# DMA transposes of one head at a time with two buffers each way, the last pair turned on TensorE, and new numbers in the scheduler

## The chip, the cores and the metric

One core of a Trainium2 chip runs the whole program. The metric is device time in microseconds (us), the median of three runs. A profile of one more execution shows what each engine did: PE (TensorE matmuls), PEld (its weight loads), DVE (VectorE), ACT (ScalarE), POOL (GpSimd) and SP, the engine that issues every DMA here.

## The reference

Attention with a compressive memory, over 4 batches, 8 heads, 576 positions and 64 elements a head, and then one gated feed-forward layer over the 2304 rows that come out:

```python
scores = scale * np.matmul(q, k.transpose(0, 1, 3, 2))
scores = np.where(causal, -1000000000.0, scores)
a = np.exp(scores - scores.max(-1, keepdims=True))
local = np.matmul(a / (a.sum(-1, keepdims=True) + 1e-09), v)
mem_out = einsum(phi(q), M_prev) / (einsum(phi(q), z_prev) + 1e-06)
x = g * mem_out + (1 - g) * local          # g is a gate per head
...
gate = 1.0 / (1.0 + np.exp(-(x @ w_gate)))   # 512 by 1536
val = x @ w_val                              # 512 by 1536
out = gate * val @ w_out                     # 1536 by 512
```

## The kernel before, in words

**Groups and pairs.** The 2304 rows are worked on in six groups of 384. Groups 1 to 4 are the first 384 positions of a batch; groups 0 and 5 ("tails") are the last 192 positions of two batches each. A group has four pairs of heads, so there are 24 pairs, numbered 0 to 23; a pair has three items of 128 query rows.

**Attention of a pair.** `scores` multiplies queries and keys on PE into a PSUM bank, reduces them on DVE into `a` (with the running extreme in `st`), and takes the exponential on ACT. `turn` brings `a` of an item into `at`, with keys on the partitions: for pairs below `XBAR` (8) by PE transposes (`transpose`) and ACT copies; from pair 8 on through `crossed`. That one splits the 32-bit numbers into two planes of 16 bits on DVE (into `pl`), has SP issue a DMA transpose (`tl<-pl`), and puts the planes together on DVE (`at<-tl`). `values` multiplies `at` with the values (tiles `vt` and `vr`) on PE, `scaled` divides, the memory term is added (`xs`), and `across` transposes `xs` on PE into `xh` and `xl`, high and low parts of the expert's input. An item has one block of 128 keys, two or three in groups 1 to 4; in group 5 it has four, four and five (the fifth half filled).

**Expert.** `moe(g)` runs over 12 slices of 128 hidden columns. A slice takes 24 matmuls with 384 columns (`wg` and `sv` with `xh` and `xl`) and nine with 512 columns (`sv` with `gh` and `gl`). The weights are converted once, in group 0, from 64-bit numbers that are loaded into `wr`, written to a scratch tensor and loaded again as `sv` in each later group. Attention of group g + 1 is laid beside `moe(g)`; the first slice of a group puts the blocks of x that come last (those of the fourth pair) at its end. Group 0's attention has almost no expert work beside it, and the last group's expert work has no attention beside it.

**Order.** All instructions go through `Program.add`, with an engine, a cost in us, what is read and written, and `kb` for transfers. `Program.issue` plays the program through by these costs: on each engine it takes the ready instruction with the lowest place in the program, less a `LEAD` by part and engine. What comes out is the order on each engine, and each engine runs it in that order and waits where its data is not there. So a cost that is changed moves instructions on all engines. SP too issues in that order; a transfer that waits for its source holds up those behind it.

**Buffers of the turn.** `pl` and `tl` are rings (`Ring`) of one buffer each, 2048 numbers of 16 bits wide. They lie in `wr0` and `wr1`, which nobody needs any more when the weights are converted.

Of the kernel before, what the change touches and what calls it, by code (L numbers as in the profile page):

```python
# [29 lines left out]

LEAD = {("attention", "pe"): 150, ("weights", "sp"): 200}

# [9 lines left out]
class Program:  # L42
# [7 lines left out]
    def __init__(self):  # L50
        self.ops = []
        self.writer = {}
        self.readers = {}
        self.touched = {}
        self.before = {}
        self.part = ""
        self.turn = None

    def renew(self, key):

        last = self.touched.get(key)
# [87 lines left out]
def tile_attention_memory_moe(  # L149
# [26 lines left out]
    class Ring:  # L176
# [10 lines left out]
        def take(self):  # L187
            i = self.at % self.n
            self.at += 1
            tag, lies = self.tags.get(i, (f"{self.name}{i}", None))  # L190
            k = pg.renew(lies or (self.name, i))
            if i not in self.tiles:
                self.tiles[i] = sb.tile(self.shape, self.dtype, name=f"{self.name}{i}", tag=tag)
                if self.init:
                    self.init(self.tiles[i], k)
            return self.tiles[i], k
# [11 lines left out]
    def pe(cost, emit, r, w):  # L208
        pg.add("pe", cost, emit, r, w)
# [5 lines left out]
    def product(out, lhsT, rhs, n, r, w, start, stop):  # L215
        pe(0.06 if n <= 100 else 4 * n / 2385.0,
           lambda: nc.tensor.matmul(out=out, lhsT=lhsT, rhs=rhs, start=start, stop=stop), r, w)  # L217
# [73 lines left out]
    def pad(t, k):  # L291
# [14 lines left out]
    vt_r = Ring("vt", [128, 5, 2, VC], F32, 2)  # L306
    kp_r = Ring("kp", [128, 2 * GT], F32, 4)
    kq_r = Ring("kq", [128, 2 * GT], F32R, 5,
                {0: ("wr2", ("wr", 2)), **{i + 1: (f"wt{i}", ("wt", i)) for i in range(4)}})
    ql_r = Ring("ql", [128, GT], F32R, 2, init=half)  # L310
    a_r = Ring("a", [128, 640], F32, 5, init=pad)
    st_r = Ring("st", [128, 2], F32, 6)
    at_r = Ring("at", [128, 1280], F32, 4)
    pl_r = Ring("pl", [128, 4 * DM], U16, 1, {0: ("wr0", ("wr", 0))})
    tl_r = Ring("tl", [128, 4 * DM], U16, 1, {0: ("wr1", ("wr", 1))})
    xs_r = Ring("xs", [128, 3, 2, D], F32, 2)
# [138 lines left out]
    def scores(n, c):  # L455
# [8 lines left out]
        def part(i, k0, k1):  # L464
# [32 lines left out]
        for (aj, ak), (sj, sk) in zip(a, st):  # L497
            act(W, lambda aj=aj, sj=sj: nc.scalar.activation(  # L498
                out=aj[:, :W], in_=aj[:, :W], func=AF.Exp, scale=-1.0, bias=sj[:, len(ns) - 1:len(ns)],
            ), [ak, sk], [ak])  # L500
        u.a[c] = a

    def crossed(a, nb, at, k):


        W = 128 * nb
        keys = []
        for js in [(0, 1)] if nb < 5 else [(0,), (1,)]:
            m = len(js)
            pl, pk = pl_r.take()  # L510
            tl, lk = tl_r.take()
            pks = [pk + (j,) for j in js]
            for x, j in enumerate(js):
                t, ak = a[j]
                src = t[:, :W].bitcast(U16).rearrange("p (w two) -> p two w", two=2)
                dst = pl[:, 2 * W * x:2 * W * (x + 1)].rearrange("p (two w) -> p two w", two=2)
                dve(2 * W, lambda src=src, dst=dst: nc.vector.tensor_copy(out=dst, in_=src),  # L517
                    [ak] + [ak[:2] + (ak[2], "pad")] * (nb == 5), [pks[x]], fast=True)
            src, dst = pl[:, :2 * W * m], tl[:, :2 * W * m].rearrange("p (x q) -> p x q", q=128)
            pg.add("sp", 0.5, lambda src=src, dst=dst: nc.sync.dma_start_transpose(out=dst, in_=src),  # L520
                   pks, [lk], 1.05 * W * m)
            src = tl[:, :2 * W * m].rearrange("p (m two w) -> p m two w", m=m, two=2)
            dst = at[:, W * js[0]:W * js[0] + W * m].bitcast(U16).rearrange("p (m w two) -> p m two w", m=m, two=2)
            if m == 1:
                src, dst = src[:, 0], dst[:, 0]
            key = k + (js[0],)
            dve(2 * W * m, lambda src=src, dst=dst: nc.vector.tensor_copy(out=dst, in_=src), [lk], [key], fast=True)  # L527
            keys.append(key)
        return keys

    def turn(n, c):
# [60 lines left out]

    def attn():
        load_pair(0)
        gates()
        load_values(0)
# [252 lines left out]
```

## Time and profile before

| | before |
|---|---|
| median of three runs | 682.6 us (682.58 to 683.85) |
| profiled execution, its own time | 682.01 us |
| span of its instructions | 680.2 us |
| PE busy | 644.5 us (95%) |
| PEld busy | 561.6 us (83%) |
| DVE busy | 428.9 us (63%) |
| ACT busy | 297.9 us (44%) |
| POOL busy | 12.1 us (2%) |
| mean granted TensorE clock | 0.982 |

The span goes from the first instruction to the last; the execution's own time is 1.8 us longer. A busy share is a mean over all stages. Matmuls overlap in the records, so that a busy PE says only that it was not waiting. In tables by stretch each engine has its busy us and, in brackets, its number of instructions, in the order PE, PEld, DVE, ACT, POOL; behind them stand the granted TensorE clock (1.00 is 2.4 GHz, 0.50 is 1.2 GHz), the mean busy share of the 16 DMA engines, and GB/s. In a timeline "xN" is a run of N like instructions, and square brackets give the idle time of the engine before it and what ended it.

### The profile page before, as it was taken

The numbers are of one execution on the slowest core, as the hardware profiler recorded it, in microseconds if no ns is written. First come the engines' busy times: TensorE is split into PE (matmuls) and PEld (weight loads), VectorE is DVE, ScalarE is ACT, GpSimd is POOL, SyncE is SP. The second block draws the span as 40 slices with busy tenths as digits, with TensorE's granted clock in tenths as the row PEclk, the third lists the DMA queues.
The fourth block names the chain that finished last, engine by engine and source line by source line (L and its number), as shares of the span: only waits on it lengthen the run. The fifth ranks groups of instructions, "written<-read, shape, count | busy, mean of one in ns | idle before, by whom it ended". The sixth has DMA issues, their size and how long they took to land.

```text
span 680.2 us, 12091 instructions
## 1 busy us (share of the span) xinstructions
PE 644.5 (95%) x4744; PEld 561.6 (83%) x4744; DVE 428.9 (63%) x1110; ACT 297.9 (44%) x580; POOL 12.1 (2%) x52
## 2 busy tenths in 40 slices
PE   4999999999999999999999999999999999289997
PEld 2556688888799999999998998988998987279996
DVE  6787879889837755666676476578467675321112
ACT  5777657648625433543344344336234333011111
POOL 2000000000000000000000000000000000000000
PEclk9999999999999999999999999999999999579999
DMA  8777748877797657786776988677976769304542
GB/s 292 257 245 239 223 137 282 269 261 247 207 254 206 191 167 236 228 188 198 202 194 178 265 214 198 175 209 242 240 192 187 192 184 266 70 10 177 186 147 85
DMA packets 97097, 138.44 MB, mean 204 GB/s; under 512 B 72720, under 2 KB 74768, under 8 KB 87824
## 3 DMA queue, kind: packets, MB, share of 16 engines
q1 hardware_dynamic: 97040, 137.67, 68.3%
q8 instruction: 37, 0.61, 0.4%
q14 instruction: 20, 0.16, 0.1%
HBM read 104.09 MB, written 17.30 MB: 178 GB/s over the span
## 4 chain that ended last, share of the span: by engine, by line
PE 90%; DVE 4%; DMA 3%; ACT 1%; issue 1%
PE bank L213 71%; PE bank L217 10%; PE bank L477 5%; PE bank L220 3%; DMA tl<-pl 2%; DVE a L489 1%; DVE pl L517 1%; DMA wr<-in_w_dram 1%; ACT a L498 1%; DVE at L527 1%; DMA kp<-in_qk_dram 0%; DVE kq L236 0%; DVE xs L236 0%; ACT xh L226 0%; DVE gl L236 0%
## 5 line engine op out<-in xcount | busy, mean ns | idle before, releaser
L213 PE MATMUL bank<-xh,wg 128*128 128x384 f32 x576 | 166.0, 344 | 0.6 <-ACT xh L226 0.6
L213 PE MATMUL bank<-xh,sv 128*128 128x384 f32 x576 | 163.2, 340 | 0.0
L213 PE MATMUL bank<-sv,gh 128*128 128x512 f32 x432 | 139.7, 399 | 0.0
L725 DVE SCALAR_TENSOR_TENSOR th<-th,bank 128x384 f32<-128x384 f32 x72 | 39.8, 552 | 124.1 <-PE bank L213 117.6
L213 PEld LDWEIGHTS bank<-xh,wg 128*128 128x128 f32 x576 | 106.3, 190 | 5.8 <-issue 1.7
L213 PEld LDWEIGHTS bank<-xh,sv 128*128 128x128 f32 x576 | 105.6, 188 | 2.2 <-issue 1.6
L498 ACT ACTIVATE a<-a,st 128x512 f32<-128x512 f32 (+4 forms) x144 | 81.9, 583 | 39.2 <-DVE st L489 38.5
L213 PE MATMUL bank<-xl,wg 128*128 128x384 f32 x288 | 98.6, 342 | 0.0
L213 PE MATMUL bank<-xl,sv 128*128 128x384 f32 x288 | 98.4, 342 | 0.0
L213 PEld LDWEIGHTS bank<-sv,gh 128*128 128x128 f32 x432 | 79.0, 188 | 13.8 <-issue 1.8
L723 ACT ACTIVATE th<-bank 128x384 f32<-128x384 f32 x72 | 35.3, 490 | 125.4 <-PE bank L213 125.4
L213 PE MATMUL bank<-sv,gl 128*128 128x512 f32 x216 | 86.0, 398 | 0.0
L226 ACT CAST gh<-th 128x384 fp32r<-128x384 f32 x72 | 36.8, 512 | 105.4 <-DVE th L725 105.3
L489 DVE CUSTOM_DVE_ANT_0 a<-bank,mask 128x128 f32<-128x128 f32 (+4 forms) x144 | 68.5, 486 | 14.4 <-PE bank L213 5.9
L226 ACT CAST kq<-kp 64x768 fp32r<-64x768 f32 (+1 forms) x76 | 48.0, 638 | 27.3 <-PE bank L213 25.9
L527 DVE COPY at<-tl 128x512 uint16<-128x512 uint16 (+4 forms) x52 | 45.1, 867 | 21.8 <-DMA tl<-pl 21.5
L213 PEld LDWEIGHTS bank<-xl,wg 128*128 128x128 f32 x288 | 54.7, 190 | 3.4 <-issue 0.5
L213 PEld LDWEIGHTS bank<-xl,sv 128*128 128x128 f32 x288 | 54.3, 188 | 1.2 <-issue 0.7
L236 DVE TENSOR_TENSOR gl<-th,gh 128x384 fp32r<-128x384 f32 x72 | 40.0, 556 | 22.0 <-ACT gh L226 21.4
L477 PE MATMUL bank<-kp 64*128 64x512 f32 (+5 forms) x156 | 44.1, 491 | 8.8 <-DMA kp<-in_qk_dram 8.8
L213 PEld LDWEIGHTS bank<-sv,gl 128*128 128x128 f32 x216 | 40.6, 188 | 8.4 <-issue 0.2
L517 DVE COPY pl<-a 128x256 uint16<-128x256 uint16 (+4 forms) x96 | 44.2, 495 | 0.1
(65 smaller groups left out, 716.6 us busy)
## 6 DMA issues: line engine op xcount, KB each, us to landing
sv<-w SPq DMA_DIRECT2D x60, 1024.0 KB, 5.1
wr<-in_w_dram SPq DMA_DIRECT2D x36, 512.0 KB, 4.8
kp<-in_qk_dram SPq DMA_DIRECT2D x32, 384.0 KB, 5.0
w<-sv SPq DMA_DIRECT2D x12, 1024.0 KB, 5.8
out_dram<-ob SPq DMA_DIRECT2D x14, 256.0 KB, 5.5
vt<-in_vp_dram SPq DMA_DIRECT2D x8, 330.0 KB, 4.8
vr<-in_vp_dram SPq DMA_DIRECT2D x8, 330.0 KB, 4.1
vt<-in_vp_dram SPq DMA_DIRECT2D x8, 198.0 KB, 2.9
```

The costliest lines, as they stand in the source:

```text
L213: lambda: nc.tensor.matmul(out=out, lhsT=lhsT, rhs=rhs, start=start, stop=stop), r, w)
L217: lambda: nc.tensor.matmul(out=out, lhsT=lhsT, rhs=rhs, start=start, stop=stop), r, w)
L220: pe(0.110, lambda: nc.tensor.transpose(out=out, in_=in_, identity=identity), r, w)
L226: act(n, lambda: nc.scalar.copy(out=out, in_=in_), r, w)
L236: dve(n, lambda: nc.vector.tensor_tensor(out=out, in0=in0, in1=in1, op=op), r, w)
L477: pe(2 * m / 2385.0, lambda kp=kp, j=j, r=r, q=q, m0=m0, m1=m1: nc.tensor.matmul(out=sp[j][0][m0:m1, :m], lhsT=kp[r, u.qa + q:u.qa + q + m ...
L489: dve(m + 60, lambda aj=aj, sj=sj, pj=pj: nc.vector.tensor_tensor_reduce(out=aj[:, k0:k1], in0=pj[:, :m], in1=mk, scale=-0.125, scalar=3.0 ...
L498: act(W, lambda aj=aj, sj=sj: nc.scalar.activation(out=aj[:, :W], in_=aj[:, :W], func=AF.Exp, scale=-1.0, bias=sj[:, len(ns) - 1:len(ns)], ...
L517: dve(2 * W, lambda src=src, dst=dst: nc.vector.tensor_copy(out=dst, in_=src), [ak] + [ak[:2] + (ak[2], "pad")] * (nb == 5), [pks[x]], fas ...
L527: dve(2 * W * m, lambda src=src, dst=dst: nc.vector.tensor_copy(out=dst, in_=src), [lk], [key], fast=True)
L723: act(GT, lambda: nc.scalar.activation(out=th, in_=pg_[:, :GT], func=AF.Tanh, scale=0.5), [pg_k], [th_k])
L725: dve(GT, lambda: nc.vector.scalar_tensor_tensor(out=th, in0=th, scalar=1.0, in1=pv[:, :GT], op0=ALU.add, op1=ALU.mult,), [th_k, pv_k], [t ...
```

## The change

- `crossed` turns one head at a time: two DMA transposes for an item where there was one (or, for an item of five blocks, two of five blocks), each with its own copy out. `pl` and `tl` become rings of two buffers of half the width; both halves of `pl` lie in `wr0` and both of `tl` in `wr1`.
- The fifth block of a tail's item goes through PE transposes and an ACT copy (key `"end"`).
- The last pair (23) is turned on PE, as pairs 0 to 7 are.
- The loads of pair 0's keys and queries (`kp`) get a lead of 1000 on SP, and stand ahead of the first weights.
- Costs in the scheduler: a narrow product 0.068 for 0.06, score matmuls of the first nine pairs up by 0.07 or 0.21 each, exponentials by 0.1 (120 columns), the issue of a DMA transpose 1.3 for 0.5, and its transfer 1.5 KB a column of a head for 1.05.
- The rings' keys are tracked so that a buffer laid into another's place has its own name; nothing is computed in another way.

```diff
-LEAD = {("attention", "pe"): 150, ("weights", "sp"): 200}
+LEAD = {("attention", "pe"): 150, ("weights", "sp"): 200, ("first", "sp"): 1000}
...
-        pe(0.06 if n <= 100 else 4 * n / 2385.0,
+        pe(0.068 if n <= 100 else 4 * n / 2385.0,
...
-    pl_r = Ring("pl", [128, 4 * DM], U16, 1, {0: ("wr0", ("wr", 0))})
-    tl_r = Ring("tl", [128, 4 * DM], U16, 1, {0: ("wr1", ("wr", 1))})
+    pl_r = Ring("pl", [128, 2 * DM], U16, 2, {i: (plain, "wr", 0) for i in range(2)})
+    tl_r = Ring("tl", [128, 2 * DM], U16, 2, {i: (turned, "wr", 1) for i in range(2)})
...
-                        pe(2 * m / 2385.0, lambda kp=kp, j=j, r=r, q=q, m0=m0, m1=m1: nc.tensor.matmul(
+                        pe(2 * m / 2385.0 + (0.07 if pair else 0.21), lambda kp=kp, j=j, r=r, q=q, m0=m0, m1=m1: nc.tensor.matmul(
...
-            act(W, lambda aj=aj, sj=sj: nc.scalar.activation(
+            act(W + 120, lambda aj=aj, sj=sj: nc.scalar.activation(
...
-        W = 128 * nb
+        n = min(nb, 4)
+        W = 128 * n
         keys = []
-        for js in [(0, 1)] if nb < 5 else [(0,), (1,)]:
-            m = len(js)
+        for j, (t, ak) in enumerate(a):
             pl, pk = pl_r.take()
             tl, lk = tl_r.take()
...
-            pg.add("sp", 0.5, lambda src=src, dst=dst: nc.sync.dma_start_transpose(out=dst, in_=src),
-                   pks, [lk], 1.05 * W * m)
...
+            pg.add("sp", 1.3, lambda pl=pl, tl=tl: nc.sync.dma_start_transpose(
+                out=tl.rearrange("p (x q) -> p x q", q=128), in_=pl), [pk], [lk], 1.5 * W)
...
+        if nb > n:
+            tp, tk = bank("att")
+            for j, (t, ak) in enumerate(a):
+                transpose(tp[:, j * 128:j * 128 + 128], t[:, W:W + 128], idn,
+                          [ak, "idn", ak[:2] + (ak[2], "pad")], [tk])
+            key = k + ("end",)
+            copy(at.rearrange("p (j x) -> p j x", j=2)[:, :, W:W + 128],
+                 tp[:, :256].rearrange("p (j x) -> p j x", j=2), 256, [tk], [key])
             keys.append(key)
...
-        if n >= XBAR:
+        if XBAR <= n < NP - 1:
...
+        pg.part = "first"
         load_pair(0)
+        pg.part = "attention"
```

**Where instructions stand.** The first transfers on SP, before (`wr` are weights, `kp` keys and queries, `bt` the gate's numbers):

```order
L244 DMA wr_129<-in_w_dram 128x1024
L244 DMA wr_131<-in_w_dram 128x1024
L244 DMA wr_133<-in_w_dram 128x1024
L244 DMA kp_101<-in_qk_dram 128x768
L244 DMA kp_102<-in_qk_dram 128x768
L244 DMA bt<-in_beta_dram 128x8
```

and of the change (its line 256 is line 244 of before):

```order
L256 DMA kp_101<-in_qk_dram 128x768
L256 DMA kp_102<-in_qk_dram 128x768
L256 DMA wr_129<-in_w_dram 128x1024
L256 DMA wr_131<-in_w_dram 128x1024
L256 DMA wr_133<-in_w_dram 128x1024
L256 DMA bt<-in_beta_dram 128x8
```

The two loads of pair 0 went ahead of three weight loads; from `bt` on the first 19 transfers stand as before.

On PE, where the last pair's attention ends, before (`kq` and `ql` are its last scores; `vr` with `at` its values; bank_66 and bank_67 with `xh_154` the first slice of the last group):

```order
L213 MATMUL bank_66<-xh_154,wg_89 128x384
L213 MATMUL bank_67<-xh_154,sv_128 128x384
L213 MATMUL bank_67<-xl_155,sv_128 128x384
L213 MATMUL bank_67<-xh_154,sv_128 128x384
L213 MATMUL bank_68<-kq_164 128x256
L213 MATMUL bank_68<-kq_164,ql_161 128x256
L213 MATMUL bank_68<-kq_162 64x256
L213 MATMUL bank_68<-kq_162,ql_161 64x256
L217 MATMUL bank_69<-vr_110,at_127 64x66 x16
L217 MATMUL bank_69<-vr_111,at_137 64x66 x16
```

and of the change (lines 225, 229 and 232 are 213, 217 and 220 of before; `a` is what is transposed; `xh_140` belongs to the group before the last):

```order
L225 MATMUL bank_67<-xl_141,sv_150 128x384
L232 MATMUL bank_68<-idn,a_118 128x128
L232 MATMUL bank_68<-idn,a_119 128x128 x3
L225 MATMUL bank_67<-xh_140,sv_150 128x384 x2
L225 MATMUL bank_67<-xl_141,sv_150 128x384
L225 MATMUL bank_67<-xh_140,sv_150 128x384
L225 MATMUL bank_63<-sv_145,gh_148 128x512 x2
L229 MATMUL bank_70<-vr_110,at_127 64x66 x16
L229 MATMUL bank_70<-vr_111,at_137 64x66 x16
```

The last pair's values stood behind everything else that PE could do, with only the rest of the last group after them; now they stand inside the last two slices of the group before, and the 26 new transposes of that pair lie in runs of one to four between its matmuls. A little further on, with the pair's `xs`:

```order
L225 MATMUL bank_65<-sv_145,gl_149 128x512
L225 MATMUL bank_63<-sv_150,gh_152 128x512 x2
L225 MATMUL bank_63<-sv_150,gl_153 128x512
L232 MATMUL bank_68<-idn,xs_143 128x128 x3
L225 MATMUL bank_64<-sv_150,gh_152 128x512 x2
L225 MATMUL bank_64<-sv_150,gl_153 128x512
L225 MATMUL bank_65<-sv_150,gh_152 128x512 x2
L225 MATMUL bank_65<-sv_150,gl_153 128x512
L225 MATMUL bank_66<-xh_154,wg_89 128x384
```

Ten matmuls with 512 columns now stand between the last value product and the transposes of `xs`, and six of them and 18 of the next group's first slice behind those, ahead of the first that needs them.

In groups 1 to 4 SP had one transpose for an item, as here:

```order
L520 DMA_TRANSPOSE tl_159<-pl_158 128x12x128
L244 DMA sv_128<-w_80 128x2048
L520 DMA_TRANSPOSE tl_159<-pl_158 128x4x128
L244 DMA vt_103<-in_vp_dram 128x396
L244 DMA sv_145<-w_81 128x2048
```

and has two of the change, between the same loads:

```order
L530 DMA_TRANSPOSE tl_wr_159<-pl_wr_158 128x6x128 x2
L256 DMA out_dram<-ob_156 64x512 x2
L256 DMA sv_128<-w_80 128x2048
L530 DMA_TRANSPOSE tl_wr_159<-pl_wr_158 128x2x128 x2
L256 DMA vt_103<-in_vp_dram 128x396
```

There are 52 DMA transposes before, and 90 of the change; PE has 32 transposes more.

## Rows read from the trace of the kernel before

**Rows 1.** stretches of the whole program: us, then busy us (instructions) by engine
```profile
8.26:85.00 76.74, 71.56 (x753) 44.70 (x753) 63.24 (x194) 55.88 (x112) 1.67 (x12) 1.00 0.74 248
85.00:570.97 485.97, 485.67 (x3479) 437.14 (x3477) 334.89 (x857) 221.52 (x432) 6.01 (x20) 1.00 0.74 213
...
577.00:600.30 23.30, 6.82 (x109) 5.75 (x108) 9.03 (x16) 1.60 (x3) 0.00 (x0) 0.59 0.30 59
600.30:605.30 5.00, 5.00 (x15) 4.57 (x16) 1.65 (x3) 1.01 (x2) 0.00 (x0) 0.50 0.00 0
605.30:675.30 70.00, 69.91 (x365) 64.83 (x363) 12.98 (x24) 11.88 (x25) 0.00 (x0) 1.00 0.38 136
```

**Rows 2.** what PE's matmuls waited for: us in total, times, longest us
```profile
PE bank L477 <- DMA kp<-in_qk_dram: 8.8, 2, 8.3
PE bank L217 <- issue: 7.5, 2, 5.7
PE bank L217 <- DVE at L527: 6.5, 2, 3.6
```

**Rows 3.** timeline before the last group: start us, us, engine, line, instruction
```profile
579.97 12.68 SPq L520 DMA_TRANSPOSE tl<-pl  x3
584.27 1.31 DVE L527 COPY at<-tl 128x2048 uint16<-128x2048 uint16 x1 [4.33 <-DMA tl<-pl]
...
595.59 1.37 PE L217 MATMUL bank<-vr,at 128*64 128x66 f32 x20 [3.61 <-DVE at L527]
...
598.83 0.90 PE L220 MATMUL bank<-idn,xs 128*128 128x128 f32 x3 [1.88 <-DVE xs L236]
...
600.30 0.69 PE L213 MATMUL bank<-xh,wg 128*128 128x384 f32 x1 [0.57 <-ACT xh L226]
```

**Rows 4.** stretch 570.97 to 605.30, only the matmuls of L213
```profile
570.97:605.30 34.33, 10.24 (x43) 8.85 (x44) 0.65 0.41 92
```

**Rows 5.** chain that ended last, two pieces: start us, us, what
```profile
16.60 1.05 PE bank L477 x2
...
533.43 3.18 PE bank L217 x104
```

**Rows 6.** timeline of PE in the middle and before the hole
```profile
345.09 0.49 PE L220 MATMUL bank<-idn,xs 128*128 128x128 f32 x3
345.33 0.48 PE L213 MATMUL bank<-sv,gh 128*128 128x512 f32 x1
...
571.25 0.34 PE L213 MATMUL bank<-xh,wg 128*128 128x384 f32 x1
571.42 0.34 PE L213 MATMUL bank<-xh,sv 128*128 128x384 f32 x1
```

**Rows 7.** timeline of the first 24 us
```profile
0.74 1.34 SPq L244 DMA_DIRECT2D wr<-in_w_dram  x3
...
4.74 0.66 ACT L639 ACTIVATE wt<-wr 128x512 f32<-128x512 f32 x1 [2.72 <-DMA wr<-in_w_dram]
...
7.31 3.69 SPq L244 DMA_DIRECT2D mb<-in_mz_dram  x4
...
8.26 3.52 PE L477 MATMUL bank<-kp 64*128 64x512 f32 x8 [8.26 <-DMA kp<-in_qk_dram]
...
16.10 0.39 PE L217 MATMUL bank<-mb,ph 128*128 128x130 f32 x2
```

**Rows 8.** loads of tile mb in the first 20 us
```profile
DMA to landing us min/median/max: 5.3/6.5/7.5
```

**Rows 9.** tile tl: durations ns min/median/max, and from issue to landing
```profile
L520 SPq DMA_TRANSPOSE tl<-pl x52: 1190/1366/7332, 175.2 to 591.3; - x52
L527 DVE COPY at<-tl x52: 455/890/1367, 185.3 to 594.7; 128x512 uint16<-128x512 uint16 x12, 128x1024 uint16<-128x1024 uint16 x12, 128x1536 uint16<-128x1536 uint16 x12, 128x2048 uint16<-128x2048 uint16 x8
...
DMA to landing us min/median/max: 2.4/4.9/9.4
```

**Rows 10.** tile at, copies from PSUM: ns min/median/max
```profile
L226 ACT COPY at<-bank x44: 353/577/599, 13.9 to 166.5; 128x512 f32<-128x512 f32 x32, 128x256 f32<-128x256 f32 x12
```

More of the change, by code (lines that the diff above doesn't have):

```diff
@@ L55, in __init__ @@
         self.before = {}
+        self.closed = set()
         self.part = ""
@@ L59, in renew @@
     def renew(self, key):
+        assert key not in self.closed, f"{key} has a new tenant"
         last = self.touched.get(key)
@@ L189, in take @@
             self.at += 1
-            tag, lies = self.tags.get(i, (f"{self.name}{i}", None))
-            k = pg.renew(lies or (self.name, i))
+            k = pg.renew((self.name, i))
             if i not in self.tiles:
-                self.tiles[i] = sb.tile(self.shape, self.dtype, name=f"{self.name}{i}", tag=tag)
+                home = self.tags.get(i)
+                if home:
+                    hosts, ring, at = home
+                    if hosts[at] is None:
+                        hosts[at] = sb.tile([128, hosts["wide"]], self.dtype, name=f"{self.name}_{ring}{at}", tag=f"{ring}{at}")
+                    place = sum(1 for j in self.tiles if self.tags.get(j) == home) * self.shape[1]
+                    self.tiles[i] = hosts[at][:, place:place + self.shape[1]]
+                    pg.before[(self.name, i)] = set(pg.touched[(ring, at)][1]) | pg.before[(self.name, i)]
+                    pg.closed.add((ring, at))
+                else:
+                    self.tiles[i] = sb.tile(self.shape, self.dtype, name=f"{self.name}{i}", tag=f"{self.name}{i}")
                 if self.init:
@@ L307, in tile_attention_memory_moe @@
     kp_r = Ring("kp", [128, 2 * GT], F32, 4)
+    in_wr, in_wt = {"wide": 2 * GT, 2: None}, {"wide": 2 * GT, **dict.fromkeys(range(4))}
+    plain, turned = {"wide": 4 * DM, 0: None}, {"wide": 4 * DM, 1: None}
     kq_r = Ring("kq", [128, 2 * GT], F32R, 5,
-                {0: ("wr2", ("wr", 2)), **{i + 1: (f"wt{i}", ("wt", i)) for i in range(4)}})
+                {0: (in_wr, "wr", 2), **{i + 1: (in_wt, "wt", i) for i in range(4)}})
     ql_r = Ring("ql", [128, GT], F32R, 2, init=half)
@@ L503, in crossed @@
     def crossed(a, nb, at, k):
-        W = 128 * nb
+        n = min(nb, 4)
+        W = 128 * n
         keys = []
-        for js in [(0, 1)] if nb < 5 else [(0,), (1,)]:
-            m = len(js)
+        for j, (t, ak) in enumerate(a):
             pl, pk = pl_r.take()
             tl, lk = tl_r.take()
[L512 to L519, printed above, removed]
-            pg.add("sp", 0.5, lambda src=src, dst=dst: nc.sync.dma_start_transpose(out=dst, in_=src),
-                   pks, [lk], 1.05 * W * m)
[L522 to L527, printed above, removed]
@@ new lines, in crossed @@
+            pl, tl = pl[:, :2 * W], tl[:, :2 * W]
+            src = t[:, :W].bitcast(U16).rearrange("p (w two) -> p two w", two=2)
+            dve(2 * W, lambda src=src, pl=pl: nc.vector.tensor_copy(
+                out=pl.rearrange("p (two w) -> p two w", two=2), in_=src), [ak], [pk], fast=True)
+            pg.add("sp", 1.3, lambda pl=pl, tl=tl: nc.sync.dma_start_transpose(
+                out=tl.rearrange("p (x q) -> p x q", q=128), in_=pl), [pk], [lk], 1.5 * W)
+            dst = at[:, 128 * nb * j:128 * nb * j + W].bitcast(U16).rearrange("p (w two) -> p two w", two=2)
@@ new lines, in crossed @@
+            key = k + (j,)
+            dve(2 * W, lambda tl=tl, dst=dst: nc.vector.tensor_copy(
+                out=dst, in_=tl.rearrange("p (two w) -> p two w", two=2)), [lk], [key], fast=True)
+            keys.append(key)
+        if nb > n:
[6 more added lines that the diff above has]
+                 tp[:, :256].rearrange("p (j x) -> p j x", j=2), 256, [tk], [key])
```

## The prediction

> **What bounds the kernel now.** I read the table by stretches first. From 85.00 to 570.97 PE is busy 485.67 of 485.97 us at a clock of 1.00 [rows 1]: there PE is the bound, the other engines have slack (DVE 334.89 of 485.97), and an edit is worth what it adds to or takes from PE. Two places are different. Before 8.26 PE does nothing, and from there to 85.00 it is idle 5.2 us (76.74 less 71.56) [rows 1]; the waits of PE's matmuls say that the 8.26 is a wait for the first keys [rows 2]. And from 577.00 to 605.30 the rest is lost: 6.82 busy us in 23.30 at a mean clock of 0.59, and then 5.00 us at 0.50 [rows 1]. The timeline of that hole shows who holds PE: three DMA transposes of the last pair one after another, each followed by a copy of DVE that waited for it, then value products that waited for the copy, the pair's `xs`, and at 600.30 the first expert matmul that needs it [rows 3]. Nothing else was left for PE: the group before had run out, and so had those 18 matmuls of the next first slice that don't need the fourth pair. From 605.30 on PE runs 365 matmuls in 70.00 us without a gap [rows 1], and stores end the program; neither is touched.
>
> **How large the hole is.** From 570.97, where the values of pair 22 end, to 605.30 pass 34.33 us. The useful work in it at full clock: 43 matmuls of L213 [rows 4], at the 0.17 us from one start to the next that full-clock neighbours show (571.25, 571.42) [rows 6], 7.3; 104 value products in 3.2, as for an earlier pair [rows 5]; six transposes, at three in 0.24 (345.09 to 345.33) [rows 6], 0.5. Together 11.0, so 23.3 us are lost. Of these 2.4 are the clock alone: 15 matmuls in 5.00 us [rows 1] would take 2.6.
>
> **The last pair on PE** takes that hole away, if PE has other work while the pair's chain runs. In the new order the pair's values stand inside the last two slices of the group before; ten matmuls with 512 columns cover the way from its values to its `xs` (at some 0.23 each, by 0.17 for 384 columns, 2.3 us; in the hole that way took from 596.96, where the products ended, to 598.83 [rows 3], 1.9), and six more and the 18 of the next slice cover the rest. I take back all 23.3, and leave 1.0 for waits in that stretch: none at the least, and at most those of the second rival below. PE never falls idle for long, so I expect the clock to stay at 1.00.
>
> **Added work on PE.** 26 transposes for the last pair and six for the fifth blocks of pairs 20 to 22. In the steady stretch one costs 0.08 us [rows 6]; some stand alone or in twos, so I take 0.09, and 2.9 in all. Bounds: 2.6 at 0.08, and 9.6 if each took the 0.30 of the three at half clock (0.90) [rows 3], to which I give little, since these run at full clock. The Trainium skill, "TensorE: Matmul & The Clock Gate", Part 4: PE-mode transpose, gives about 275 ns for one of 128 by 128 inside a kernel, and would make this term 8.8 and the time 667; the spacing of 0.08 here decides against it, so it has no chance of its own below. The ten copies to `at` that go with them take ACT 0.58 each [rows 10], 5.8 us of an engine that is busy 221.52 of 485.97 [rows 1]; only the last one stands on a path, and its cover is the six expert matmuls ahead of the values.
>
> **Halves instead of whole items** for pairs 8 to 22. SP issues 90 transposes for 52; at 1.37 us each [rows 9] the 38 more cost SP 52 us, spread over the 416 from the first to the last [rows 9]. Behind a transpose that waits for DVE stand weight loads, and PE waits for these; the cover is that `sv` has three buffers. DVE makes 38 copies more out of `tl`, each at half the width; even at the shortest now, 0.46, [rows 9] that is 17 us less the wider ones that go, inside 151 us of slack. From issue to landing a transpose takes 2.4 to 9.4 us, 4.9 in the median, over sizes of one to four [rows 9], so a half is hardly quicker than the whole, but with two buffers the second is on its way 1.4 us behind the first. I take nothing for all this; it gains nothing because PE doesn't wait there, and what it can cost is the first rival. The Trainium skill speaks against cutting transfers, in "DMA: Bandwidth & Descriptors", by its two cost components: about 2.0 us fixed, and then bytes over 436 GB/s. The shortest landing here, 2.4, agrees with it; 38 more would be 76 us of waiting if they stood one behind another on the path, and 661 would become 737.
>
> **First keys first.** The first weights landed at 4.74, when ACT took them up, 4.0 us after SP's first issue; the keys behind three weight loads let PE start at 8.26 [rows 7]. In their place the keys land by about 4.4 (they are smaller), so PE starts 3.9 earlier at the most. But bytes ahead of the later loads are the same, and the memory term that follows needs `mb`, issued in four parts from 7.31 on, in 3.69 us [rows 7], and landing 5.3 to 7.5 later [rows 8], the last near 15.5; PE used it at 16.10 [rows 7]. There PE meets the data again. By then the change has put two more score matmuls, 1.05 us [rows 5], ahead of it, and the remaining wait is 0.6 to 1.0 shorter: I take 2.0. The ends are 0 and 3.9. On DVE and ACT the first conversions move back by some 2 us behind the first scores; these weights are wanted only when group 0's expert work starts.
>
> **Other costs** move instructions on every engine. Where PE is full that can't help; up to 85.00 there are 5.2 idle us to win, or as many to lose if a wait moves. I take 0, with 2 either way.
>
> **The sum** against the profiled execution: 682.0 − 23.3 + 1.0 + 2.9 − 2.0 = 660.6. That execution is 0.6 below the median of the runs, so 661.2, and I say **661**.
>
> **Rivals.** *The halves come late* (the other side). If the second half waits for the first to land, an item's turn is longer by up to 4.9 − 1.4 = 3.5 us [rows 9], and the third item of each of 15 pairs (8 to 22) is the one that its values wait for. For: landing does not shrink with size, and the order leaves the values little beyond the time that the scheduler assumes. Against: the halves have a buffer each, and PE hardly waits now from 85.00 to 570.97 (0.3 us) [rows 1] with landings as uneven as 2.4 to 9.4. All of it would be 15 × 3.5 = 52 us: 713, slower. It decides from 1.4 us a pair on, where 15 × 1.4 eats the 21.4 won. In a mild form, the three tail pairs alone waiting 2 to 3 us, it gives 668.
>
> *The last pair's chain is not covered.* If the group before is through earlier than the order assumes, PE still waits for the pair: for the way from values to the first expert matmul, 596.96 to 600.30 [rows 3], 3.3; a copy of 0.6 [rows 10]; and reduction and exponential ahead of it, which I estimate at as much again as the way behind. That is 7 us where I left 1: 667. For it: all of it is one serial chain. Against: 10, 6 and 18 matmuls stand in its gaps.
>
> *The change does not empty the hole*, because pairs 20 to 22, still turned by DMA, end as late as they did: then only the last pair's own three waits go (7.5 and 6.5 us of idle time [rows 2]) less the transposes: about 670.
>
> *The first keys give nothing*: 663; *or all*: 659.
>
> **How the numbers follow.** The forecast with either end of the first keys 0.70; the uncovered chain 0.12; late halves, mild, 0.07; a hole that stays in part 0.05; late halves in all pairs 0.04; no change within 0.2% (1.4 us, about what runs of this kernel tell from nothing) 0.02. From the terms the forecast's own range is 656 (all of the keys, nothing left to wait, 2 won early) to 665; up to 669 it takes in the uncovered chain and the mild late halves, and that leaves out about 1 in 10. Faster 0.94, same 0.02, slower 0.04.
>
> **What the profile after would show.** Hole: no stretch of clock 0.50 behind 85 us, and no idle time of PE above 1 us between the pair's last scores and the last group's first slice; value products of the last pair waiting for ACT's copy, if for anything. Keys: PE's first matmul near 4.4, its first with `mb` near 15, and the first expert matmul about 2 us earlier. Transposes: 0.08 to 0.11 apart. Halves: PE's idle time in the middle still under 1 us, with landings near 4 and SP waiting less for `tl<-pl`. The prediction is wrong if PE waits for copies out of `tl` at the values of pairs 8 to 22, or if weight loads land late behind waiting transposes.

## The result and the profile after

The changed kernel takes **659.37 us** (median of 4 runs, 657.28 to 662.13), the kernel before 682.59 in the runs beside it. The ratio is 0.966, 95% interval [0.962, 0.970]: faster by 3.4%. The profiled execution took 662.13 us, the slowest of the four; its span is 660.3. The forecast was 661, in a range of 656 to 669.

The page of after, engine totals and then busy tenths and granted clock in 40 slices of the span:

```profile
PE 639.6 (97%) x4776; PEld 561.7 (85%) x4776; DVE 423.2 (64%) x1142; ACT 303.9 (46%) x590; POOL 9.1 (1%) x52
...
PE   5998999999999999999999999999999999999996
...
PEclk9899989999999999999999999999999999999999
```

Each digit is a slice of 16.5 us. There is no hole in the tail any more; the clock is below 9 tenths only in the second and the sixth slice. The windows of after, cut at its own events (us, PE busy, instructions, granted clock, DMA share, GB/s), answer to [rows 1]:

```profile
0.00:8.26 8.26, 4.37 (x11) 1.00 0.74 253
8.26:12.24 3.98, 3.51 (x27) 1.00 0.90 334
12.24:15.95 3.71, 0.00 (x1) 0.93 1.08 259
15.95:20.00 4.05, 4.05 (x12) 0.50 0.95 325
20.00:85.00 65.00, 59.11 (x699) 0.97 0.74 242
85.00:565.27 480.27, 478.65 (x3469) 1.00 0.75 211
565.27:579.41 14.14, 14.14 (x173) 1.00 0.18 64
579.41:600.30 20.89, 20.78 (x113) 1.00 0.61 213
600.30:654.95 54.65, 54.65 (x286) 1.00 0.39 139
```

Two things stand here. From 565.27 on, where 22 of the last pair's 26 transposes begin (four ran at 547.94), PE is never idle for more than 0.11 us in a row of the table, at full clock; before, 23.30 us held 6.82 busy ones at 0.59. And the start has a new gap: 3.71 us without work, and behind it 4.05 us at 0.50. The 1.00 in the first row is no reading: the trace of after has no entry of the clock before 8.60 us, and where there is none the table prints 1.00. What PE's matmuls waited for in the whole program (us in total, times, longest; the first three) answers to [rows 2]:

```profile
PE bank L491 <- DMA kp<-in_qk_dram: 7.6, 2, 3.8
PE bank L491 <- DVE xs L248: 1.7, 2, 0.9
PE bank L225 <- ACT xh L238: 1.4, 1, 1.4
```

The waits of value products for copies out of the transposed tile (6.5 and 7.5 before) are gone. The wait for first keys is now two, 3.8 at the start of the program and 3.7 for the second pair's keys. PE's timeline in the tail (start, us, instruction) answers to [rows 3]; L225, L229 and L232 are L213, L217 and L220 of before:

```profile
568.26 0.60 PE L232 MATMUL bank<-idn,a 128*128 128x128 f32 x4
568.62 0.42 PE L225 MATMUL bank<-xh,sv 128*128 128x384 f32 x1
568.88 0.60 PE L232 MATMUL bank<-idn,a 128*128 128x128 f32 x4
...
569.49 0.34 PE L225 MATMUL bank<-xl,sv 128*128 128x384 f32 x1
569.67 0.34 PE L225 MATMUL bank<-xh,sv 128*128 128x384 f32 x1
...
571.55 0.62 PE L225 MATMUL bank<-sv,gh 128*128 128x512 f32 x2
572.10 3.25 PE L229 MATMUL bank<-vr,at 128*64 128x66 f32 x104
...
577.68 0.49 PE L232 MATMUL bank<-idn,xs 128*128 128x128 f32 x3
...
579.41 0.33 PE L225 MATMUL bank<-xh,wg 128*128 128x384 f32 x1
```

The reader sees the pair's chain laid into expert matmuls: transposes in fours, the 104 value products at 572.10, `xs` at 577.68, and the last group from 579.41. No row has a wait in brackets. `xs` stands 21.15 us earlier than the 598.83 of [rows 3]. Four transposes take 0.36 (568.26 to 568.62), and the matmul behind them 0.26 to the next start (568.62 to 568.88) where one between matmuls takes 0.18 (569.49 to 569.67): 0.44 for a run of four, 0.11 each.

The turned tile of after (durations ns min/median/max, first and last start; from issue to landing) answers to [rows 9]:

```profile
L530 SPq DMA_TRANSPOSE tl_wr<-pl_wr x90: 1167/1220/3065, 169.4 to 549.0; - x90
...
DMA to landing us min/median/max: 2.3/4.8/8.5
```

In the median a half lands no sooner than a whole did (4.9), with two buffers and so at times two transposes under way. The first 20 us, SP's issues and then PE, answer to [rows 7, 8]:

```profile
0.73 0.88 SPq L256 DMA_DIRECT2D kp<-in_qk_dram  x2
1.65 1.38 SPq L256 DMA_DIRECT2D wr<-in_w_dram  x3
...
4.89 1.38 SPq L256 DMA_DIRECT2D kp<-in_qk_dram  x2
7.88 4.85 SPq L256 DMA_DIRECT2D mb<-in_mz_dram  x4
```

```profile
3.85 3.78 PE L491 MATMUL bank<-kp 64*128 64x512 f32 x8 [3.85 <-DMA kp<-in_qk_dram]
...
15.95 2.08 PE L491 MATMUL bank<-kp 64*128 64x512 f32 x4 [3.71 <-DMA kp<-in_qk_dram]
17.96 0.80 PE L229 MATMUL bank<-mb,ph 128*128 128x130 f32 x2
```

PE begins 4.4 us earlier than before and then stands still for the second pair's keys; `mb` is used at 17.96, not at 16.10. The first eight scores take 3.78, near the pace of the four behind the gap, which take 2.08 at 0.50.

### The profile page after: what moved, and what is told of

It reads as the page before. It is cut to its first block, busy times and chain, and to the rows that moved or that the text cites. A ratio compares the mean times of both kernels' runs of the same rounds, so it can differ in the third digit from the quotient of the medians.

```text
span 660.3 us, 12262 instructions
## 1 busy us (share of the span) xinstructions
PE 639.6 (97%) x4776; PEld 561.7 (85%) x4776; DVE 423.2 (64%) x1142; ACT 303.9 (46%) x590; POOL 9.1 (1%) x52
## 4 chain that ended last, share of the span: by engine, by line
PE 86%; DMA 6%; DVE 4%; ACT 2%; issue 1%; SPq 1%; ACTq 0%; DVEq 0%
PE bank L225 72%; PE bank L229 8%; PE bank L491 3%; DMA kp<-in_qk_dram 3%; PE bank L232 3%; DMA wr<-in_w_dram 2%; DMA tl_wr<-pl_wr 2%; DVE a L503 1%; SPq L256 1%; DVE wt L662 0%; ACT a L512 0%; DVE wt L665 0%; DVE ql L248 0%; DVE kq_wt L248 0%; DVE xl L248 0%
## 5 line engine op out<-in xcount | busy, mean ns | idle before, releaser
L225 PE MATMUL bank<-xh,wg 128*128 128x384 f32 x576 | 165.4, 342 | 1.9 <-ACT xh L238 1.4
L225 PE MATMUL bank<-xh,sv 128*128 128x384 f32 x576 | 164.2, 341 | 0.2 <-DVE th L744 0.2
L225 PE MATMUL bank<-sv,gh 128*128 128x512 f32 x432 | 142.9, 400 | 0.0
L225 PEld LDWEIGHTS bank<-xh,wg 128*128 128x128 f32 x576 | 105.3, 188 | 8.7 <-issue 2.1
L225 PEld LDWEIGHTS bank<-xh,sv 128*128 128x128 f32 x576 | 104.9, 188 | 2.3 <-issue 1.1
L225 PE MATMUL bank<-xl,sv 128*128 128x384 f32 x288 | 98.2, 341 | 0.0
L225 PE MATMUL bank<-xl,wg 128*128 128x384 f32 x288 | 97.6, 339 | 0.2 <-DVE xl L248 0.2
L225 PEld LDWEIGHTS bank<-sv,gh 128*128 128x128 f32 x432 | 78.9, 188 | 12.1 <-issue 0.8
L225 PE MATMUL bank<-sv,gl 128*128 128x512 f32 x216 | 86.0, 398 | 0.0
L225 PEld LDWEIGHTS bank<-xl,wg 128*128 128x128 f32 x288 | 54.3, 189 | 3.4 <-issue 0.5
L534 DVE COPY at<-tl_wr 128x256 uint16<-128x256 uint16 (+3 forms) x90 | 46.5, 519 | 14.0 <-DMA tl_wr<-pl_wr 13.6
L225 PEld LDWEIGHTS bank<-xl,sv 128*128 128x128 f32 x288 | 54.1, 188 | 1.2 <-issue 0.7
L238 ACT CAST kq_wt<-kp 64x768 fp32r<-64x768 f32 (+2 forms) x60 | 38.1, 637 | 24.7 <-PE bank L225 22.8
L225 PEld LDWEIGHTS bank<-sv,gl 128*128 128x128 f32 x216 | 40.6, 188 | 8.5 <-issue 0.7
L491 PE MATMUL bank<-kp 64*128 64x512 f32 (+5 forms) x156 | 38.1, 511 | 9.8 <-DMA kp<-in_qk_dram 7.6
L528 DVE COPY pl_wr<-a 128x256 uint16<-128x256 uint16 (+3 forms) x90 | 41.8, 469 | 0.1
```

The costliest lines, as they stand in the source:

```text
L238: act(n, lambda: nc.scalar.copy(out=out, in_=in_), r, w)
L491: pe(2 * m / 2385.0 + (0.07 if pair else 0.21), lambda kp=kp, j=j, r=r, q=q, m0=m0, m1=m1: nc.tensor.matmul(out=sp[j][0][m0:m1, :m], lhsT= ...
L528: dve(2 * W, lambda src=src, pl=pl: nc.vector.tensor_copy(out=pl.rearrange("p (two w) -> p two w", two=2), in_=src), [ak], [pk], fast=True)
L534: dve(2 * W, lambda tl=tl, dst=dst: nc.vector.tensor_copy(out=dst, in_=tl.rearrange("p (two w) -> p two w", two=2)), [lk], [key], fast=True)
```

## The experiments

Beside the first four of the table the kernel before took 683.01 us, beside the next four 683.70, beside the last four 683.52; from one four to another the ratios compare best.

| run | us | ratio to before, 95% |
|---|---|---|
| after again | 658.26 | 0.963 [0.9615, 0.9652] |
| weights first | 659.15 | 0.965 [0.9628, 0.9668] |
| two pairs first | 661.21 | 0.968 [0.9645, 0.9710] |
| last pair alone | 668.15 | 0.977 [0.9753, 0.9791] |
| last pair by DMA | 664.75 | 0.972 [0.9698, 0.9743] |
| whole items | 686.05 | 1.003 [1.0013, 1.0044] |
| old numbers | 657.15 | 0.962 [0.9598, 0.9643] |
| weights last | 658.18 | 0.964 [0.9612, 0.9658] |
| halves, one buffer | 774.62 | 1.132 [1.1290, 1.1343] |
| whole items, old price | 656.81 | 0.960 [0.9573, 0.9620] |
| halves and PE alone | 662.28 | 0.969 [0.9667, 0.9715] |
| old numbers, weights last | 655.09 | 0.959 [0.9571, 0.9617] |

### The tail: which edit closes the hole

**The last pair alone**, on top of the kernel before:

```diff
-        if n >= XBAR:
+        if XBAR <= n < NP - 1:
```

> The kernel before with one edit: the last pair is turned by transposes on PE, nothing else. Theory that the closed hole is the whole gain and this edit alone closes it: 682.6 - 23.3 + 1.0 + 26 x 0.109 = 663.1 us, and no stretch of clock 0.50 after 85 us. Rival: whole items with one buffer and the old cost numbers keep pairs 20 to 22 late, so that the last pair still finds PE without other work: a hole of 7 to 10 us stays, 668 to 672 us.

668.15: the rival's time. PE's timeline of this run where the pair ends:

```profile
579.39 0.34 PE L213 MATMUL bank<-xh,sv 128*128 128x384 f32 x1
579.57 2.41 PE L220 MATMUL bank<-idn,a 128*128 128x128 f32 x14
581.90 3.25 PE L217 MATMUL bank<-vr,at 128*64 128x66 f32 x104
587.11 0.55 PE L220 MATMUL bank<-idn,xs 128*128 128x128 f32 x3 [1.95 <-DVE xs L236]
588.22 0.44 PE L213 MATMUL bank<-xh,wg 128*128 128x384 f32 x1 [0.57 <-ACT xh L226]
```

The last expert matmul that doesn't need the pair is the one at 579.39. From 579.57 to 588.22, 8.65 us, PE has only the pair's own chain; 14 transposes at 0.11, the 104 products in 3.25 and `xs` are some 5 of them. The hole is smaller, but it is not closed: this is the prediction's own rival of a chain that is not covered (667).

**The last pair by DMA**, on top of after, in halves like the others:

```diff
-        if XBAR <= n < NP - 1:
+        if n >= XBAR:
```

> The changed kernel with the last pair turned by DMA again, in halves and with two buffers each way, like pairs 8 to 22. Theory that the transposes on PE are what closes the hole: PE waits again for the last pair's values, 659.0 - 26 x 0.109 (2.8) + 6 to 23 us = 662 to 679, likeliest 666, with PE idle behind 570 us and a stretch of clock 0.50. Rival: the halves and the earlier last pair alone close it, since the pair's scores now stand inside the expert work of the group before: no hole, and 2.8 us less than after, 656.

664.75, some 6 us more than after again (6.5 by the times, 5.9 by the ratios). What PE waited for behind 560 us, and two windows:

```profile
PE bank L229 <- DVE at L534: 4.5, 1, 4.5
PE bank L232 <- DVE xs L248: 1.9, 1, 1.9
```

```profile
560.00:580.00 20.00, 14.97 (x164) 0.95 0.75 209
580.00:600.00 20.00, 18.09 (x81) 0.80 0.15 53
```

PE waits for the copy out of the transposed tile again, and the clock falls, to a mean of 0.80. So the transposes on PE are worth some 6 us where everything else is in place, and 14.9 (683.01 less 668.15) alone. The rest of the change gains 19.0 (683.70 less 664.75) without them, the start's share among it. The hole can be closed once; the parts overlap.

**Whole items**, on top of after: both heads in one transpose, one buffer each way, fifth blocks by DMA, at the new numbers.

```diff
-    pl_r = Ring("pl", [128, 2 * DM], U16, 2, {i: (plain, "wr", 0) for i in range(2)})
-    tl_r = Ring("tl", [128, 2 * DM], U16, 2, {i: (turned, "wr", 1) for i in range(2)})
+    pl_r = Ring("pl", [128, 4 * DM], U16, 1, {i: (plain, "wr", 0) for i in range(1)})
+    tl_r = Ring("tl", [128, 4 * DM], U16, 1, {i: (turned, "wr", 1) for i in range(1)})
...
-        for j, (t, ak) in enumerate(a):
+        for js in [(0, 1)] if nb < 5 else [(0,), (1,)]:
...
+            pg.add("sp", 1.3, lambda src=src, dst=dst: nc.sync.dma_start_transpose(out=dst, in_=src),
+                   pks, [lk], 1.5 * W * m)
```

> The changed kernel with whole items again (both heads of an item in one DMA transpose, one buffer each way, the fifth blocks of pairs 20 to 22 turned by DMA in a transpose of their own), with the new cost numbers, the first keys first and the last pair on PE. The prediction gave the halves nothing: 659.0 - 6 x 0.109 = 658.4. Rival, from the run with only the last pair on PE, which left about 5 us of waits between 574 and 589 us: without the halves the order leaves the last pair behind the expert work of its group, so these waits are back, 664 to 669.

686.05: all the gain is gone (1.003 of before), and the time is beyond the rival's range. PE's longest wait behind 560 us:

```profile
PE bank L229 <- DVE at L541: 10.7, 2, 7.0
```

Is it the chip, too slow with whole items, or the order that the scheduler makes for them? **Whole items at the old price** sets back one price of that run, the DMA transpose's, which has two numbers:

```diff
-            pg.add("sp", 1.3, lambda src=src, dst=dst: nc.sync.dma_start_transpose(out=dst, in_=src),
-                   pks, [lk], 1.5 * W * m)
+            pg.add("sp", 0.5, lambda src=src, dst=dst: nc.sync.dma_start_transpose(out=dst, in_=src),
+                   pks, [lk], 1.05 * W * m)
```

> The run with whole items (686) with one number set back: the DMA transpose's cost in the scheduler's model, 0.5 on SP and 1.05 per column in place of 1.3 and 1.5. If whole items are too slow on the chip (landing and one buffer), it stays at 680 to 688 with PE waiting for copies out of the transposed tile. Rival: what made 686 is the order that the scheduler draws from the higher number; at the lower number the last pair's scores and transposes stand inside the expert work again, and the chip keeps up: 659 to 663.

656.81, the rival's cause and even under its range. The same transposes, of the same size, with one buffer, and nothing is lost. From issue to landing in this run, and PE's longest wait behind 85 us:

```profile
DMA to landing us min/median/max: 2.4/4.8/7.8
```

```profile
PE bank L225 <- ACT xh L238: 0.6, 1, 0.6
```

So 29 us hang on a price that no instruction contains. In the order at 1.3 and 1.5, the values of pair 22 (570.92) and with them nearly all of the last pair stand behind the last matmul with 512 columns of the group before the last (569.43); at 0.5 and 1.05 pair 22 and the last pair's scores and transposes stand ahead of it.

**Halves with one buffer** each way, on top of after:

```diff
-    pl_r = Ring("pl", [128, 2 * DM], U16, 2, {i: (plain, "wr", 0) for i in range(2)})
-    tl_r = Ring("tl", [128, 2 * DM], U16, 2, {i: (turned, "wr", 1) for i in range(2)})
+    pl_r = Ring("pl", [128, 2 * DM], U16, 1, {i: (plain, "wr", 0) for i in range(1)})
+    tl_r = Ring("tl", [128, 2 * DM], U16, 1, {i: (turned, "wr", 1) for i in range(1)})
```

> The changed kernel with halves, but one buffer each way. If it is the cutting that counts (two short transposes in place of a long one), the time stays at 659. Rival: it is the second buffer: with one, the scheduler's model lets the pairs' transposes follow each other, and its order puts the whole last pair behind the expert work of its group, as with whole items at the new numbers (686): 680 to 688, with PE idle behind 560 us.

774.62, far beyond both. The tile and who waited for it, then PE's longest waits behind 85 us:

```profile
L530 SPq DMA_TRANSPOSE tl_wr<-pl_wr x90: 1167/1210/2032, 164.1 to 668.5; - x90
...
  DVE at L534: 79.5, 37
```

```profile
PE bank L229 <- DVE at L534: 43.8, 16, 5.4
```

90 transposes, none issued before the one ahead has landed, span 504 us from the first to the last; with two buffers the 90 of after fit into 380, since 43 of them are issued before the one ahead has landed. The 504 hold other waits too, so 5.7 a step (89 steps) is not what one costs. Where five stand in a row, they take 15.12 with the last one's issue of 1.2, some 3.5 a step:

```profile
284.74 15.12 SPq L530 DMA_TRANSPOSE tl_wr<-pl_wr  x5
```

At the new price, halves with one buffer are a loss, and the second buffer makes up for it. The order of this run also leaves the last pair behind, as that of whole items does, and its share isn't taken apart. Halves with one buffer at the old price were not run, so how much of the loss is the chip's and how much the order's is not shown. The Trainium skill, "DMA: Bandwidth & Descriptors", two cost components, puts the fixed part of a transfer that GpSimd issues at about 2.0 us, and 42 more transposes in a row would be 84 (an estimate from it). Over whole items at the same price and with one buffer (686.05) it is 88.6 here; the orders of the two runs differ too, so the trace agrees in size, but doesn't show that this is the cause.

**Halves and PE alone**: the kernel before with halves, two buffers, last pair and fifth blocks on PE, old numbers, weights first.

```diff
-LEAD = {("attention", "pe"): 150, ("weights", "sp"): 200, ("first", "sp"): 1000}
+LEAD = {("attention", "pe"): 150, ("weights", "sp"): 200}
...
-        pe(0.068 if n <= 100 else 4 * n / 2385.0,
+        pe(0.06 if n <= 100 else 4 * n / 2385.0,
```

(against after; the other numbers as in the run with old numbers below)

> The kernel before with the halves, two buffers each way, and the last pair and the fifth blocks on PE, but with all old cost numbers and the weights ahead of the first keys. If these two edits are the whole change: 657 to 659, no wait of PE above 1 us behind 85 us. Rival: the first keys first are worth the 2.0 of the prediction: 659 to 660, against 657.2 of the same kernel with the keys first.

662.28, 21.2 less than before: all of the tail's gain, and no matmul of PE waits behind 560 us. But it is 3.3 above the 659 of the first theory and beyond the rival too, so the rest of the change is worth some us at the start.

### The start and the numbers

**After again**, unaltered:

> The changed kernel once more, unaltered, so that the edits beside it have a run on the same chip, and to see whether the start in the profile of after (second pair's keys landing at 15.82 and 16.75 us, PE idle for 3.71 us, clock 0.50 from 15.95 to 20.00) belongs to the program or to that one execution. If to the program: the same wait within 0.5 us, and the second keys again after 15 us. If to that execution: the keys land near 13 to 14.5 us as they did before the change, the wait is under 2 us. Time in either case 657 to 662 us.

658.26 (657.43 to 659.11). The second keys landed at 14.24 and 15.73 here (15.82 and 16.75 in the first profile) and PE waited 2.22 for them, so the wait is in part the program's and in part that execution's; the two windows of this run behind 12 us, then one further on:

```profile
12.00:16.00 4.00, 1.47 (x6) 0.90 1.15 274
16.00:20.00 4.00, 3.21 (x13) 0.50 0.97 355
...
85.00:90.00 5.00, 5.00 (x28) 1.00 0.04 14
```

The low clock behind the wait is there again. A dip to 0.79 between 85 and 90 us, in after's first profile, is not.

Both executions run the same instructions in the same order, so their traces can be laid side by side. After's first profile is 0.7 us behind this one at 22.9 us, 1.6 at 64.4 (ACT takes up a later load of keys at 62.17, here at 59.22), 2.5 at 82.1 (PE waits 1.4 for `xh`, here 0.4) and 3.8 at 86.6 (48 value products at 0.50 take 2.91, here 1.62). So the second keys are the smaller part of what sets the two apart.

**Weights first**, on top of after (the diff of `LEAD` above):

> The changed kernel with the first three weight loads ahead of the first keys again. Forecast of the prediction: the first keys gain 2.0 us, so this one takes 661.4. Rival, from the profile of after: PE starts 4.4 us earlier and then waits 3.7 us for the second pair's keys, so the edit gains nothing and this one takes 659.4 within 1 us. In both, PE's first matmul near 8.3 us.

659.15: the rival's time. Against after again it is 0.9 more, and the intervals overlap, so a gain between nothing and 2 is not ruled out. With the old numbers the same edit is another matter: 662.28 (halves and PE alone) against 657.15, 5.1 us, with intervals apart. The **old numbers**, on top of after:

```diff
-        pe(0.068 if n <= 100 else 4 * n / 2385.0,
+        pe(0.06 if n <= 100 else 4 * n / 2385.0,
...
-                        pe(2 * m / 2385.0 + (0.07 if pair else 0.21), lambda kp=kp, j=j, r=r, q=q, m0=m0, m1=m1: nc.tensor.matmul(
+                        pe(2 * m / 2385.0, lambda kp=kp, j=j, r=r, q=q, m0=m0, m1=m1: nc.tensor.matmul(
...
-            act(W + 120, lambda aj=aj, sj=sj: nc.scalar.activation(
+            act(W, lambda aj=aj, sj=sj: nc.scalar.activation(
...
-            pg.add("sp", 1.3, lambda pl=pl, tl=tl: nc.sync.dma_start_transpose(
-                out=tl.rearrange("p (x q) -> p x q", q=128), in_=pl), [pk], [lk], 1.5 * W)
+            pg.add("sp", 0.5, lambda pl=pl, tl=tl: nc.sync.dma_start_transpose(
+                out=tl.rearrange("p (x q) -> p x q", q=128), in_=pl), [pk], [lk], 1.05 * W)
```

> The changed kernel with all the scheduler's old cost numbers (products 0.06, nothing added to the scores, exponentials W, DMA transposes 0.5 on SP and 1.05 per column). The prediction gave the numbers nothing: 659.0 within 2 us. Rival: it is the numbers that pull the last pair's scores forward into the expert work; then the waits of the last pair are back, 664 to 668.

657.15: no loss; the interval overlaps with that of after again. The new numbers help by 3.1 where the weights are first (662.28 to 659.15) and not where the keys are. PE's start with old numbers and first keys:

```profile
3.92 3.79 PE L491 MATMUL bank<-kp 64*128 64x512 f32 x8 [3.92 <-DMA kp<-in_qk_dram]
...
13.19 1.13 PE L491 MATMUL bank<-kp 64*128 64x512 f32 x4 [1.81 <-DMA kp<-in_qk_dram]
```

The four scores that took 2.08 in after take 1.13 here: the keys came at 13.15, PE had been idle for 1.81 and not for 3.71, and the clock, at 1.00 from 8.64 on, did not fall.

**Two pairs first**, on top of after:

```diff
         load_pair(0)
+        load_pair(1)
         pg.part = "attention"
         gates()
         load_values(0)
-        load_pair(1)
```

> The changed kernel with the keys of the first two pairs, not of the first alone, ahead of the weights. If the wait for the second keys (3.7 us idle, and some 2 us more by a clock of 0.50 behind it) is what ate the gain of the early start: PE does not idle after 12 us, and the time is 655 to 657 us. Rival: the memory term's data, issued later still, becomes the wait in its place, at 17 to 19 us, and the time stays at 659.4 within 1 us.

661.21, but from 657.37 to 666.10: inconclusive. In its profile the wait for second keys is gone and `mb` has one of 3.0 in its place. **Weights last** puts that ahead of the weights, too:

```diff
         load_pair(0)
-        pg.part = "attention"
+        load_pair(1)
         gates()
+        load_unit(0)
         load_values(0)
-        load_pair(1)
+        pg.part = "attention"
```

> The changed kernel with the first weights behind everything that the first two pairs need: keys of both pairs, the gates' beta, the memory term's data and the first pair's values, and then the weights. If PE's waits for the second keys (3.7 to 4.0 us) and for the memory term's data are a matter of what stands ahead of them in SP's queue (three weight loads, landing some 1.25 us apart, 3.75 us): no wait of PE above 1 us from 4 to 20 us, clock 1.00 there, and 655 to 656 us. Rival: weights that land later keep ACT and DVE busy with conversions just when the first pairs' exponentials and sums are due, and what is won before 20 us is lost before 85 us: 658 to 660.

658.18: the rival's time, but its mechanism (conversions in the way) is not shown. The theory's condition was not met: PE waits 2.8 for `mb`, and behind the wait its matmuls are slow, as these two rows show:

```profile
11.37 2.63 PE L229 MATMUL bank<-mb,ph 128*128 128x130 f32 x8 [2.80 <-DMA mb<-in_mz_dram]
...
19.04 1.30 PE L229 MATMUL bank<-mb,ph 128*128 128x130 f32 x8
```

The same eight matmuls take 2.63 and 1.30. The trace's first entry of the clock, 1.00, is at 16.31 in this run; until then the pace is half. With the **old numbers** as well:

> A candidate: the changed kernel with the old cost numbers and with the first weights behind all loads of the first two pairs. The old numbers alone took 657.2, the late weights alone 658.2. If their savings add up (about 1 and 0 against 658.3): 656 to 657. Rival: PE's first 20 us are bound by data whatever the order, so 657 to 658.

655.09, lower than either theory. Its start:

```profile
4.13 3.78 PE L491 MATMUL bank<-kp 64*128 64x512 f32 x8 [4.13 <-DMA kp<-in_qk_dram]
...
10.89 1.05 PE L229 MATMUL bank<-mb,ph 128*128 128x130 f32 x6 [0.24 <-DMA mb<-in_mz_dram]
...
15.04 1.13 PE L491 MATMUL bank<-kp 64*128 64x512 f32 x4
```

Here PE has no wait above 0.4 between 4.13 and 20 us, and the clock is at 1.00 from 8.54 on; the second pair's scores begin at 15.04, in weights last at 17.98. It is the fastest version run; its interval ends (0.9617) below that of after (from 0.9621) and touches that of after again (from 0.9615).

## Why the prediction was right, and where it was not

The time is 1.8 us under the forecast's 661.2. By its steps:

- **The hole, −23.3 + 1.0, and the transposes, +2.9.** Together −19.4. Halves and PE alone measures this sum by itself: −21.2. The size was right. No wait of 1.0 is left in that stretch, and a transpose costs 0.11 with what it does to the matmul behind it, not 0.09: 3.5 for 32. The forecast's 0.08, from three transposes, left out the slower start of that matmul. The some 275 ns that the Trainium skill gives for a PE-mode transpose inside a kernel ("TensorE: Matmul & The Clock Gate", Part 4) is how long one lasts here as well (0.27 for those from 565 to 571 us). They overlap, and in the stream one costs 0.11.
- **"The last pair on PE takes that hole away."** This step was wrong as it was put. Alone it takes 14.9 and leaves a chain without cover (668.15, the rival's size). What it needs is the order in which the pair's scores stand among the expert matmuls; halves with two buffers bring that order, and so do whole items at the old price with the other new numbers. Which of these other numbers does it was not run.
- **Halves, 0.** Right for the chip (whole items at the old price: 656.81), and for the reason given: PE hardly waits there (1.6 us idle from 85.00 to 565.27 in the first profile, 1.1 of waits in after again, where the forecast had under 1; none of it for the transposed tile). SP's issue took 1.22 in the median for the 1.37 told. Not right as a step that can be left out: at the new price without the second buffer the order falls apart (686.05 and 774.62). In the run with one buffer PE waits for the copies as the rival of late halves has it (43.8 us); that two buffers are why this did not happen is likely, but the price was not set back there. "Landing does not shrink with size" holds of the medians only: the shortest landing goes from 4.2 for the widest to 2.3 for the narrowest (last section).
- **First keys first, −2.0, and other numbers, 0 ± 2.** Together −2.0. From halves and PE alone (662.28) to after again (658.26) it is −4.0. Each edit alone does most of it or more (−5.1 and −3.1), so they cannot be added. The start of PE came as told (3.85 for 4.4). The first profile alone would say that the rest failed: `mb` first used at 17.96 and not near 15, and the first expert matmul at 65.91, before at 65.36. It is the exception. After again, the last pair by DMA, whole items, and whole items at the old price have the same order on PE in their first 160 us; there the first `mb` stands at 16.79, 15.99, 15.26 and 15.98, and the first expert matmul at 64.30, 63.68, 63.42 and 64.03, 1.1 to 1.9 earlier than before, near the 2 of the forecast. The second keys land at 14.24, 13.59, 13.28 and 13.54 there. In four runs with the weights first (before, the last pair alone, halves and PE alone, weights first) they land at 13.13, 13.63, 13.09 and 14.15. So later loads kept their times within what executions differ by anyway.
- **Clock at 1.00.** Right from 565 us on. At the start it was not thought of: 3.71 us without work were followed by 0.50. "No stretch of clock 0.50 behind 85 us" failed in the first profile (0.79 from 85 to 90) and held in after again.

The time came out near the forecast, but not by its account: the tail gave 1.8 more than told, the start and the numbers 2.0 more, and which edit gives what was wrong. The 4 us between two executions of one program can be followed in their traces (after again, above); why loads land at other times stays open. So does why the first keys are worth 5.1 with old numbers and 0.9 with new ones.

## What to carry to other kernels

When several edits aim at one hole, price the hole once and say what each needs from the others; here the parts alone took 14.9 and 19.0 of some 25 us, and a right sum hid a wrong attribution. A cost number in a scheduler is an edit of its own: nearer to the traced duration was not better (SP's issue of a transpose takes 1.2 to 1.4 in the median; 1.3 lost where 0.5 did not), and one price decided between 657 and 686 us. When you cut a transfer, look for a second buffer: at the new price halves with one buffer took 116 us more than halves with two. And take more than one profile of a start: one execution of this program misled by 4 us.

## What the runs showed of the hardware

- At most eight DMAs of the SP queue are in flight at any time, over the whole program, in every run. Issue and landing (us) of some of after's first loads, worked out from the trace's DMA records:

```
issued   landed
0.73     3.80   kp
1.65     7.80   wr
2.12     9.05   wr
2.60    10.44   wr
4.89    15.82   kp, second pair
7.88    17.27   mb, first part
9.07    17.61   mb
10.50   17.84   mb
```

These parts of `mb` are issued 0.02 to 0.08 us after a load has landed (7.80, 9.05, 10.44). So `mb` was late because eight loads stood ahead, not because SP is slow to issue; before, its first part at 7.31 [rows 7] follows a landing at 7.23. Whether the chip or the program's own counters hold it at eight is not settled.
- The shortest landing of a DMA transpose shrinks with its size; the medians hardly do. By the width that is turned the shortest is 2.3 us for 128x256, 2.4 for 128x512, 2.7 for 128x768 and 3.0 for 128x1024 (halves, one buffer), and 4.2 for 128x2048 (whole items, old price). In the median halves with two buffers take 4.8 and whole items (old price) 4.8; with one transpose in flight at a time, as whole items have it too, halves take 3.9.
- The granted clock fell to 0.50 behind an idle time of 3.71 us at the start, where PE had worked some 8 us before, and not behind one of 1.81 (old numbers); the same four matmuls took 2.08 and 1.13. It fell in after again too, behind idle times of 2.22 and 1.10 with four scores between, and in whole items at the old price behind 1.75 and 1.18. So the length of one idle time doesn't tell the two apart.
- When the full pace begins differs between executions. The first entry of the clock, 1.00, stands at 8.60 us in after, 8.36 in after again, 11.38 in before, 14.53 in weights first, 16.31 in weights last and 16.58 in the last pair alone; until then the spacing of matmuls is that of 0.50. No run takes apart what this is worth.
